# Three blocks of u in batch 0 turned by DMA instead of TensorE, under a new order of all engines

## The chip, the core and the metric

The kernel runs on one core of a Trainium2 chip. The core has a tensor engine (PE, with its weight loads shown apart as PEld), a vector engine (DVE), a scalar engine (ACT), a general engine (POOL) and SyncE (SP), which here issues every DMA. The metric is the device time in microseconds. Before the change the median of four runs is 229.05 us (228.66 to 229.83).

## What is computed

Inputs q, k and v are 4 batches x 8 heads x 768 positions x 64. The first half is a causal attention in which every query sees 6 chunks of 32 keys, those with the highest upper bound of the score. The second half is a mixer on the result, x (4 x 768 x 512).

```
k_min, k_max = min and max of k over each chunk of 32 positions
ub    = sum_d max(q * k_min, q * k_max)           # per query and chunk, causal
sel   = the 6 chunks with the highest ub of each query
attn  = softmax(q k^T / 8, where sel and causal)
x     = attn @ v, heads side by side
theta = x @ w_theta
z_r, z_i = x * cos(theta), x * sin(theta)
y     = w_tok_r @ z_r + w_tok_i @ z_i             # over positions
u     = x + y
out   = u + relu(u @ w_ch)
```

## The kernel before

**A recorded program in a fixed order.** `record` builds a list of some 1,390 operations ("steps" below), each with a name, an engine or a choice of engines, and the tiles that it reads and writes. The string `ORDER` (lines 17 to 77) then says in which order they are issued and, by a letter behind the number, which engine takes a step that several can do: no letter is the first choice, b the second, c the third. `decode` (line 865) turns it into a list and gives each tile its buffer. `F9` stands for nine small matmuls on zeros (line 848) that occupy PE. Each engine works through its own steps in this order, and so does SP with the DMAs: a step that waits holds up all that stands behind it on its engine. The numbers of buffers (`CLASSES`, line 107) matter for the order too: there are 6 input buffers `ld`, shared by q, k, v and weights; the scores have 2 PSUM buffers `sc`; and 3 PSUM buffers `mi` serve almost everything else.

**Names.** A step is named by kind, batch, and pair of heads (0 to 3), head (0 to 7) or block of 128 positions (0 to 5). By stages:

- Loads on SP: `Lq.b.p.x` and `Lk.b.p.x` (line 179, one half of a pair, 192 KB), `Lv.b.p` (line 187, 384 KB), weights `Lwth`, `Lwch`, `Lwtok`. Four of the six blocks of w_tok are turned by DMA (`Twtok`, line 716), the others on PE (`Tw`).
- Turns of q and k on PE, three blocks at a time (`Tq`, `Tk`, lines 231 and 434). Their evictions (`evq`, `evk`, helper lines 169 to 172) go to ACT or DVE; copies in fp16 (`cq`) and the relu of q (`relu`, lines 195 to 199) go to any of three engines.
- Bounds: `red0` and `red1` (lines 240 and 451) reduce k on DVE, `kd` takes the difference, `ub` multiplies on PE (lines 268 to 278, 491). Then DVE does `t1` (transpose), `mx` (nine maxima), `lt` (compare) and `t2` (transpose back). In batches 1 to 3, `cp` (line 536) copies the mask into rows of the q tile, on DVE, ACT or POOL.
- Scores `sc.b.h.s` on PE (line 564; in batch 0 lines 342 and 350), `ex` on ACT (exponential, line 570; 358 in batch 0), `tri` on POOL or DVE (causal triangle, line 580 or 578), `av` on PE (line 402), `norm` on DVE (lines 412 and 413), which writes a head's columns of x.
- Mixer of batch b: x is turned (`Tx` on PE with `evx` in batches 0 and 1, line 608; `Dx` by DMA in batches 2 and 3, line 600). `th.b.t` (line 617) multiplies by w_theta, `sin` and `cos` on ACT (lines 624, 628) need another table of functions than the exponential, `zr` (line 632) makes z on DVE or POOL. `mix.b.t.s` (lines 640 and 642, two matmuls each) adds up y for block t over the six z tiles in turn; `u.b.t` (line 648) adds x on DVE.
- u is turned: on PE by `Tu.b.t` (line 661, four transposes) and an eviction `evu.b.t` on DVE or ACT (line 592 or 593), or by DMA, `Du.b.t` on SP (line 654). The set `U_DMA` (line 97) says which. Then `ch.b.t` (line 673) multiplies by w_ch, `ot` on DVE (line 678) finishes the output block, and `out` on SP stores it (line 683).

The order interleaves the batches: while the mixer of one batch runs, the loads, turns, bounds and scores of the next one are put between its steps.

The two ways of turning u, in the loop over the blocks:

```
if (b, t) in U_DMA:
    op("SP", f"Du.{b}.{t}", 1270, [(u[t], 0)], [(uT[t], 0)],
       lambda t=t: nc.sync.dma_start_transpose(out=T(uT[t]).rearrange("p (c w) -> p c w", w=P), in_=T(u[t])),
       dma=900)
    continue
ps = buf("mi", f"ups.{b}.{t}", (DM,), FP16)
...
op("PE", f"Tu.{b}.{t}", 220, [(u[t], 0)], [(ps, 0)], tr)
ev16(f"evu.{b}.{t}", ps, uT[t], DM)
```

Of the kernel before, what the change touches and what calls it, by code (L numbers as in the profile page):

```python
# [15 lines left out]

ORDER = (
    "10|"
    "3 2 448 4 449b 404b 1 722b 475b 29 28 31 30 0 21 57 17 58 9 18 5 721 19b 14 7 15 56 6 F9 32 20c 10 36 55 "
    "11 35 39 48 12 F17 44 34 13b 8 41 33 85 23 45 75 16c 42 37 47b 38 22 24 84 40 25 F15 50 102 26 68 27 403 "  # L20
    "71 51 69 180 82 52 72 174 181 83 63 175 74 165 65 182 59 64 166 171 49 373 60 374 61 172 168 176b 53 115 "
    "169 67 54 F7 177 173 167b 77 62b 43 46b 170b 178 76c 95 78 125 66 206 179 191 79 96 189 207 103 188 192 "
    "200 80 183 113 208b 201 187 81 193 194 190 184 195 202 90 197 91 203 196 92 198 98 70c 86 73c 141 204 185 "
    "116 88 223 109 199 87 144 99 217 205 186 224 215 126 213 214 211 89 114 209 216 400 226 218 225 399 269 "
    "94 129 101 227 210 127 270 142 220 212 128b 104 133 110c 221 143 228b 219b 145 271 93 105 229 376 272b "
    "106 222 384 137 230 379 375 107 232 402 387 410 100 233 401 108 236 381 97 377 414 386 231 258 412b 380 "
    "234 255 146 385b 130 259 235 237 256 388 246 260 238 239 134 247 240 249 383 257 411b 241 111 250 252 153 "
    "248b 382 253 242 243 251 131 389b 474 378 413 244 273 254 263 132 267 138c 274b 135 245 262 159 266 136b "
    "265 139 268 261 390 140b 264 392 391 418 150 393 275 419 112 416 276 396b 405 394 123 277 417 408 117 "
    "422b 395 407b 162 281 409 278 154 406b 289 415b 147 160 425 155 290 420c 279 285 421c 282 161 280 283 426 "  # L30
    "124 286 435 156 297 427b 287 151 428 119 291 293 284 152 118b 315 288 299 316 429 121 298 317 292 397 295 "
    "301 430 163 302 294 436 437 318 148b 432c 446 308 434c 447 309 296 444 310 445 300 311 319 438 320 431 "
    "149 433 303 157 321 515 439 544 516 120c 304 158 122c 305 440c 347 306 443c 423 348 312 441c 307 468 313 "
    "545 517 471 528 314 343 442b 361 546 470 344b 529 557 164 362 461 463 558 462b 530 554 464b 455 398b 472 "
    "450 559 457b 560 363 465 322 451 459 473 323 452 458 324 467b 466c 494 325 453 456 326 561 454 327 424c "
    "741 345 555 534 328 460b 355 562 535 469 346 349 720 356 518 556 565 350 358 519 357 536b 481 719 359 520 "
    "476 483 563 479 547 482 717 336 477b 548 337 484 745 338 478 549 485 339 746 480 340 341 486b 718 487 342 "
    "489 488 531 495 490 364 743 532 492c 491 353 365 521 493b 541 789 533 522 564 496 742 566 354b 366 542 "
    "523 744 370 497 506 543 786 524 498 526 371 507b 734 736 787 508 329 737 330 735b 372 331 509 739b 332 "
    "499 738 788 333 740b 510 334 765 500 760 511c 335 525 761 360 728 512c 527 351 513c 730 758 352 586 729 "  # L40
    "514c 808 550 501 759 552 551 731 504c 367 587 732 764c 553 723 747 725 810 368 583 748 811 538 727 588 "
    "539 584 369 763 537 750 752 751 606 753 1053 502c 726 580 749 1054 585 755 607 733b 803 540 505c 503c 754 "
    "724b 609 608 804 756 619 762 581 621 620 790 757b 622b 766 591 793 570 792b 610 809 767 813 791b 812 582 "
    "571 794 1056 612 611 768 589 1055 590 613 777 572 573 795 592 769b 574 614 814 832 599 778b 796b 615 575 "
    "617 600 779 567 616 797 601 770 596 568 780 771 597 578 781 569 593 772 784c 576 785b 577 799 598 594 892 "
    "798 774c 618 819 800b 815 776c 898 1079 823 893 801 595 1080 579 775c 1078 899 895 894 816b 1077 802 603 "
    "900 818 885 896 807c 602 817 604 827 820b 623 886 605 882 828 879 897 624 883 903 887 625 822 805 902 880 "
    "626 1057 901 1061 884 631 821 806 904 627 633 1060 881 773 889 1058b 890 888 1059b 853 856 629 891 635 "
    "632 782 783 628 643 634 636 630 637 639 824 644 833c 647 645 638 1075 640 679 646 641 680 681 648 642 651 "
    "649 652 857 653 650 654 682 1076c 683 1120 684 1121 854 825 858 685 869 1099 655 826 855b 697 866 870 831 "  # L50
    "656 829 834 867 657 830 693 1068 835 872 868 1069 844 859 871 672 873 836 845b 837 673 1100b 874 674 846 "
    "658 860 1142 659 838 847 660 839 861 661 848 841b 699 840 851b 849 842 843b 662 852c 700 663 850c 877 701 "
    "875 664 908 918 694 909 1062 1086 1063b 876 919 910 947 1144 1090 675 1145 1089 1064 920 676 878 1087 677 "
    "1088 950 1065 864 862 1066 711 678 702 1067 712 696 1070 703 1094 1071 863 713 1095b 665 704 1073 948 865 "
    "1123 666 1081 1122 1072c 951 1092 1146 934 1084 949 1143b 1147 911 1093b 667 1166 1074 1082 668 1098b "
    "1096c 669 1085 1097 670 912 708 671 1083 1091b 935 924 952b 695 709 1101 925 913b 936b 1137 710 1102 926 "
    "905 1111 1103b 921 1138b 906 1112b 686 1104 1124 922 1135 907 1128 916 944 1105 1136 914 923b 931 1106 "
    "945 1139 915 1125b 705 1141b 917 1140 937 932 1127 687 1108c 706 927 1109c 929 1107b 688 1113 933 707 "
    "1110b 689 946 938 928 1114 1219 930 1167 1126 953 955 1213 1220 1115 939 1129 1214 954 1221 1132 1216 "
    "1117c 1133 941 1119c 1217 942 1131b 690 1215 691 956 1118c 1130 940 1218 1193 692 1226 1134b 1194 1116c "  # L60
    "1161 943 698 1148 1227 1195 1229 1162b 1222 1151 1223 1230 957 1228 1224 1149b 1232 1159 1225 1233 1153 "
    "1231 958 1206 1150 1157 1187 1234 1207 1160b 1236 1237 1156 959 1235 1188 1165c 714 1238 1154 1200 1152 "
    "961 1155 1190 715 1158b 1201 963 1189 1208 960 1191 1168 1163c 1164c 965 962 1202 1203 1169 1192 1198 "
    "1178 971 1170 1179b 716 1171 1196 964 1197 1180 967 972 973 1172 975 966 968 974 969 983 1199 976 979 977 "
    "970 985 1001 978 1002 981 1173 1003 980 1181 1004 1177 984 982 1022 1204 1023 986 1005 1182 994 1176 995 "
    "1184 996 1186 1183 1185b 1006 1174 1175b 1205 1255 1007 1258 1256 1209 1211 1031 1008 1009 1259 1257b "
    "1252 1260 1210 1253 1278 1212 997 1279 1010 1254b 1263 1239 1262 1280 1240 1261 1245 1264 998 1246 1024 "
    "1241b 1271 1025 1247 1272 1265 1026 1273b 1266 1242 1011 1243 1012 1267 1284 1027 1285 1244 1250 1281 "
    "1028 1286 1248 1249 1282 1034 1041 1251 1283 1268 1042 1013 1269 999 1043 1014 1288 1287 1270 1000 1276 "
    "1032 1289 1015 1290 1274 1275 1016 1030 1277 1017 1018 1019 1291 1020 1050 1021 1292 1044 1051 1293 1038 "  # L70
    "1045 987 1039 1294 1297 988 1299 1295 1301 989 1296 990 1298 991 1302 992 1300 1040 1305 1303 1033 993 "
    "1304b 1309 1306 1052 1307 1313 1046 1310 1029 1317 1311 1308 1314 1342 1312 1315 1343 1344 1319 1316 1345 "
    "1318 1335 1320 1336 1337 1338 1339 1340 1346 1341 1347 1328 1365 1348 1329 1330 1331 1366 1321 1322 1323 "
    "1324 1325 1326 1047 1327 1332 1048 1363 1333 1356 1334 1357 1049 1358 1359 1377 1380 1378 1364 1360 1381 "
    "1361 1379 1349 1382 1362 1350 1035 1351 1036 1352 1374 1037 1353 1375 1354 1369 1376 1355 1371 1370b 1367 "
    "1372 1389 1368b 1373 1386 1390 1383 1387 1391 1384 1388 1385 "
)

B, H, S, D = 4, 8, 768, 64
P = 128  # L80
DM = H * D
NT = S // P
CH = 32
NCH = S // CH
QS = 192
NS = S - QS
RUN = NS // 2
# [3 lines left out]
KX = D + NCH  # L91
ROW = (0,)
X_DMA = (2, 3)
K_SB = set()
LAST = (3, 4)
W_DMA = (2, 3, 4, 5)
U_DMA = {(b, t) for b in (1, 2, 3) for t in range(NT) if b < 3 or t < 4}
SEGS = [(0, 4), (1, 3), (2, 5)]
BASE = [0, 1024, 2048]

STEPS = [[(0, 0, 512)], [(0, 512, 256), (4, 512, 256)], [(1, 128, 512)], [(1, 640, 128), (3, 384, 384)],
         [(2, 256, 512)], [(5, 640, 128)]]
OFF = {0: 0, 4: 768, 1: 1024, 3: 1664, 2: 2048, 5: 2560}
# [816 lines left out]
```

## Time and profile before

| | |
|---|---|
| median of four runs | 229.05 us (228.66 to 229.83) |
| the profiled execution | 228.29 us, of which the span of the trace 226.6 us |
| clock granted to PE | 1.0 throughout |
| busy: PE, DVE, ACT, POOL | 216.0, 175.1, 164.8, 94.3 us |
| DMA | 38.06 MB, 71.2% of 16 engines' span on SP's queue |
| first y matmul of batches 0 to 3 | 52.9, 115.3, 167.8 and 199.9 us |

The trace is of one execution, so its durations are used against its own 226.6 us, and 1.7 us lie around that span. The profile's rows of tenths cut the span into 40 slices of 5.7 us; a digit is the busy share of an engine. PE counts as busy while a matmul is in flight, and matmuls overlap, so a row of nines does not say that it works at full rate: a group's mean of 379 ns for a 512-column matmul stands beside 216 ns between two that follow each other. The chain of waits is followed back from the last instruction, at each step to whatever released it. In rows of windows the columns are the window, its length, then busy time with the number of instructions for PE, PEld, DVE, ACT and POOL, the clock, the busy share of the DMA engines, and GB/s.

### The profile page before, as it was taken

Reading aid. Unit: us, or ns where it says so; the run is one execution under the profiler, and the core shown is the slowest. Engines: PE = TensorE matmul, PEld = TensorE weight load, DVE = VectorE, ACT = ScalarE, POOL = GpSimd, SP = SyncE. Lnnn points to the kernel's source line nnn. Section 1 sums busy time; section 2 is a strip of 40 time slices with the busy share of each in tenths; the row PEclk is TensorE's granted clock in tenths of the full one; section 3 lists DMA queues with packets and bytes.
Section 4 is the critical chain, followed back from the end, with each engine's and each line's share of the span. In section 5 each row is a group of like instructions: output and inputs, shape, how many; then the busy total and the mean of one; then the engine's idle time right before and its main releaser. Section 6 shows DMA issues by size and latency. Waiting matters only on the chain.

```text
span 226.6 us, 5663 instructions
## 1 busy us (share of the span) xinstructions
PE 216.0 (95%) x2122; PEld 127.3 (56%) x2122; DVE 175.1 (77%) x505; ACT 164.8 (73%) x247; POOL 94.3 (42%) x190
## 2 busy tenths in 40 slices
PE   7899999999999999888999999999989999999993
PEld 2755766843566658466645565677535564444442
DVE  4599799799979699899986899999885366342553
ACT  2659999999688758999998559899998870560011
POOL 8515557564534648958405314486501130300000
PEclk9999999999999999999999999999999999999999
DMA  7999899999999999986038479514621024662254
GB/s 160 259 258 240 267 303 250 266 319 218 296 241 209 263 247 272 249 195 141 2 72 173 124 122 242 134 48 60 108 48 23 3 69 93 94 186 46 73 173 171
DMA packets 103470, 38.06 MB, mean 168 GB/s; under 512 B 97436, under 2 KB 97820, under 8 KB 103444
## 3 DMA queue, kind: packets, MB, share of 16 engines
q1 hardware_dynamic: 103444, 37.71, 71.2%
q8 instruction: 16, 0.26, 0.5%
q14 instruction: 10, 0.08, 0.1%
HBM read 26.17 MB, written 6.29 MB: 143 GB/s over the span
## 4 chain that ended last, share of the span: by engine, by line
PE 72%; DVE 10%; ACT 8%; DMA 3%; SPq 3%; issue 2%; DVEq 0%; ACTq 0%
PE y L640 13%; PE y L642 13%; PE sc L564 9%; PE ch L673 8%; PE av L402 7%; PE th L617 5%; ACT pt L570 3%; PE qps L434 3%; SPq L600 2%; ACT pt L358 2%; PE kps L434 2%; PE ub L491 2%; DVE km L451 2%; DMA xT<-x 2%; DMA k<-in_k_dram 2%
## 5 line engine op out<-in xcount | busy, mean ns | idle before, releaser
L570 ACT ACTIVATE pt<-sc 128x1024 f16<-128x1024 f32 (+1 forms) x72 | 63.3, 919 | 8.8 <-PE sc L564 8.1
L640 PE MATMUL y<-z,wtokT 128*128 128x512 f16 x144 | 54.6, 379 | 0.1
L642 PE MATMUL y<-z,wtokT 128*128 128x512 f16 x144 | 54.5, 379 | 0.0
L580 POOL TENSOR_SCALAR_AFFINE_SELECT pt<-pt 128x256 f16<-128x256 f16 x62 | 25.6, 417 | 48.9 <-ACT pt L570 47.6
L564 PE MATMUL sc<-qx,kx 88*128 88x512 f16 (+3 forms) x192 | 37.2, 305 | 1.2 <-ACT pt L570 1.0
L402 PE MATMUL av<-v,pt 128*128 128x65 f16 x672 | 30.7, 194 | 1.3 <-ACT pt L570 0.8
L402 PEld LDWEIGHTS <-pt 128*128 128x128 f16 x672 | 27.7, 98 | 7.2 <-ACT pt L570 1.4
L648 DVE TENSOR_TENSOR u<-y,x 128x512 f16<-128x512 f32 x24 | 16.5, 689 | 14.4 <-PE y L642 14.2
L451 DVE TENSOR_REDUCE km<-kps 128x12 f32<-128x384 f32 x48 | 25.1, 546 | 1.5 <-PE kps L434 1.1
L564 PEld LDWEIGHTS <-kx 88*128 88x128 f16 x192 | 16.6, 97 | 13.2 <-issue 2.6
L617 PE MATMUL th<-wtheta,xT 128*128 128x512 f16 x96 | 22.7, 379 | 1.3 <-DMA xT<-x 0.7
L673 PE MATMUL ch<-wch,uT 128*128 128x512 f16 (+1 forms) x96 | 23.6, 374 | 0.0
L642 PEld LDWEIGHTS <-wtokT 128*128 128x128 f16 x144 | 14.1, 98 | 15.1 <-issue 0.9
L640 PEld LDWEIGHTS <-wtokT 128*128 128x128 f16 x144 | 14.0, 97 | 15.1
L678 DVE SCALAR_TENSOR_TENSOR ot<-ch,u 128x512 f32<-128x512 f32 (+1 forms) x24 | 16.3, 678 | 7.5 <-PE ch L673 7.3
L628 ACT ACTIVATE cs<-th,pi 128x512 f16<-128x512 f32 x24 | 16.5, 703 | 6.9 <-PE th L617 6.5
L358 ACT ACTIVATE pt<-sc 128x1024 f16<-128x1024 f32 (+1 forms) x24 | 20.9, 926 | 0.7 <-PE sc L350 0.7
L169 ACT COPY qT<-qps 128x384 f32<-128x384 f32 x24 | 11.2, 486 | 14.0 <-PE qps L231 7.1
L632 DVE TENSOR_TENSOR z<-x,cs 128x1024 f16<-128x1024 f16 x23 | 16.7, 743 | 5.5 <-ACT cs L628 2.7
L172 POOL CAST qx<-qT 64x768 f16<-64x768 f32 (+1 forms) x18 | 14.7, 817 | 11.7 <-ACT qT L169 6.9
L413 DVE TENSOR_TENSOR x<-av,rec 128x384 f16<-128x384 f32 x32 | 17.8, 558 | 1.1
L169 ACT CAST kx<-kps 64x384 f16<-64x384 f32 (+1 forms) x36 | 16.7, 477 | 2.3 <-PE kps L434 1.0
(103 smaller groups left out, 342.1 us busy)
## 6 DMA issues: line engine op xcount, KB each, us to landing
q<-in_q_dram SPq DMA_DIRECT2D x32, 192.0 KB, 3.7
k<-in_k_dram SPq DMA_DIRECT2D x32, 192.0 KB, 3.6
v<-in_v_dram SPq DMA_DIRECT2D x16, 384.0 KB, 4.1
out_dram<-ot SPq DMA_DIRECT2D x23, 256.0 KB, 2.3
wtok<-in_moe_w_tok_r_dram SPq DMA_DIRECT2D x6, 384.0 KB, 4.8
wtok<-in_moe_w_tok_i_dram SPq DMA_DIRECT2D x6, 384.0 KB, 4.6
wth<-in_moe_w_theta_dram SPq DMA_DIRECT2D x4, 256.0 KB, 4.4
wch<-in_moe_w_ch_dram SPq DMA_DIRECT2D x4, 256.0 KB, 4.4
```

Of the source, the lines that this page charges most:

```text
L169: c = {"A": ("ACT", int(n * 0.833 + 60), 0, lambda: nc.scalar.copy(out=out(), in_=in_())), "D": ("DVE", int(n / 0.96 + 70) if psum else in ...
L358: nc.scalar.activation(out=T(pt)[:, :, base:base + w], in_=T(ps).rearrange("p (x c) -> p x c", x=2)[:, :, 0:w], func=AF.Exp, bias=0.0, sca ...
L402: nc.tensor.matmul(ps[:, t, :], T(pt)[:, x, o:o + P], T(v16)[:, x, j, :], start=(j == 0), stop=(j == t))
L413: nc.vector.tensor_tensor(out=T(x16)[:, :, h * D:(h + 1) * D], in0=ps[:, :, 0:D], in1=T(rec).broadcast_to([P, NT, D]), op=ALU.mult)
L451: nc.vector.tensor_reduce(out=T(km)[:, j, 12 * f:12 * f + 12], in_=src.rearrange("p (c w) -> p c w", w=CH), axis=AX.X, op=o)
L564: nc.tensor.matmul(T(ps)[:, a0:a1], T(kx)[0:KX, x, j * P:(j + 1) * P], T(qx)[0:KX, x, q0 + a0 - o:q0 + a1 - o], start=True, stop=True)
L570: nc.scalar.activation(out=T(pt)[:, x, BASE[s]:BASE[s] + w], in_=T(ps)[:, 0:w], func=AF.Exp, bias=0.0, scale=SCALE)
L580: eng.affine_select(out=a, in_=a, pattern=[[0, 2], [1, P]], compare_op=ALU.is_ge, fill=G.zero_reg(), base=0, channel_multiplier=-1)
L617: nc.tensor.matmul(T(ps), T(xT[t])[:, c, :] if by_dma else T(xT[c])[:, t * P:(t + 1) * P], K.wtheta[:, c, :], start=(c == 0), stop=(c == 3))
L640: nc.tensor.matmul(T(ps), K.wtok[:, si, 0, t * P:(t + 1) * P], T(z[si])[:, 0], start=(si == 0), stop=False)
L642: nc.tensor.matmul(T(ps), K.wtok[:, si, 1, t * P:(t + 1) * P], T(z[si])[:, 1], start=False, stop=(si == NT - 1))
L673: nc.tensor.matmul(T(ps)[:, 0:n1 - n0], T(uT[t])[:, c * P:(c + 1) * P], K.wch[:, c, n0:n1], start=(c == 0), stop=(c == 3))
```

## The change

Blocks 3, 4 and 5 of batch 0 join the set whose u is turned by DMA; blocks 0, 1 and 2 of batch 0 and blocks 4 and 5 of batch 3 stay on PE. The whole `ORDER` is another one. Numbers in it shift as well, since a block turned by DMA is recorded as one step and not two.

```diff
 ORDER = (
     "10|"
-    "3 2 448 4 449b 404b 1 722b 475b 29 28 31 30 0 21 57 17 58 9 18 5 721 19b 14 7 15 56 6 F9 32 20c 10 36 55 "
-    "11 35 39 48 12 F17 44 34 13b 8 41 33 85 23 45 75 16c 42 37 47b 38 22 24 84 40 25 F15 50 102 26 68 27 403 "
+    "2 1 28 3 472b 446b 4 31 718 29 30 0 21 5 57 9 58 17 12 14 8 56 18 7 719 15 55 10 401 19b 48 6 20b F21 36 "
+    "32 11 400 16b 41 39b 13b 44 85 37 42 23 83 45 33 47b 34 38 22b 24 82 40b 35 25 F16 50 115 26 68 84 27 71 "
...
-U_DMA = {(b, t) for b in (1, 2, 3) for t in range(NT) if b < 3 or t < 4}
+U_DMA = {(b, t) for b in range(4) for t in range(NT) if (b < 3 or t < 4) and (b, t) not in ((0, 0), (0, 1), (0, 2))}
```

Decoded to names, PE's part around batch 0's mixer reads before (from its third block of y on; `mix.0.3` stands for all six steps of a block):

```
mix.0.3 Tu.0.1 sc.1.1.2 ch.0.0 Tu.0.3 sc.1.0.1 av.1.3.2 ch.0.1 Tk.1.3.1 Tk.1.3.0 av.1.3.0 sc.1.2.2 mix.0.5
Tq.1.3.0 Tq.1.3.1 sc.1.1.1 ch.0.3 Tu.0.5 sc.1.0.2 sc.1.2.0 av.1.3.1 ub.1.2 ch.0.5 av.1.0.0 av.1.0.2 Tq.2.0.0
Tq.2.0.1 mix.0.4 Tq.2.1.1 av.1.0.1 Tk.2.0.1 Tu.0.4 Tq.2.1.0 sc.1.5.2 av.1.2.0 av.1.2.2 av.1.2.1 ch.0.4 Tk.2.0.0
Tk.2.1.0 sc.1.5.1 av.1.1.1 av.1.1.2 av.1.1.0 Tk.2.1.1 sc.1.7.0 sc.1.5.0 Tq.2.2.1 sc.1.7.1 Tx.1.0 ...
```

and after:

```
mix.0.3 Tk.1.3.0 av.1.3.2 Tk.1.3.1 sc.1.1.1 av.1.3.1 sc.1.1.0 av.1.3.0 mix.0.5 (Tq.1.3.1 Tq.1.3.0 before its last)
sc.1.1.2 sc.1.2.0 ch.0.2 ub.1.2 av.1.1.1 sc.1.0.2 mix.0.4 (Tq.2.0.1 Tq.2.0.0 before its last) av.1.1.2 av.1.1.0
Tq.2.1.1 Tq.2.1.0 sc.1.5.2 Tk.2.0.1 Tk.2.0.0 av.1.2.2 av.1.2.1 av.1.2.0 sc.1.5.1 Tk.2.1.1 sc.1.5.0 Tk.2.1.0
av.1.0.0 sc.1.6.2 av.1.0.1 Tk.2.2.0 av.1.0.2 ch.0.3 sc.1.7.1 sc.1.7.2 av.1.5.1 Tx.1.0 Tx.1.1 ... Tq.2.2.1
av.1.7.1 sc.1.6.1 ch.0.5 sc.1.4.0 ch.0.4 Tk.2.3.0 ...
```

SP's part after, around the new DMAs (before, the loads follow each other in much the same way, without a Du):

```
... Lk.2.0.1 Lk.2.1.0 Lk.2.1.1 Du.0.3 Lk.2.2.0 Lk.2.2.1 Lq.2.2.0 out.0.2 Lv.2.1 Lv.2.2 Lk.2.3.0 Du.0.4 Du.0.5
Lq.2.2.1 Lq.2.3.1 Lq.2.3.0 Lk.2.3.1 out.0.3 Lq.3.0.0 ...
```

Steps that changed their engine (before to after): `cp` DVE 14 to 5, ACT 9 to 6, POOL 25 to 37; `evk` and `evq` ACT 60 to 50, DVE 28 to 38; `tri` DVE 17 to 12, POOL 79 to 84; `evu` DVE 4 to 1 (ACT 4, unchanged); fillers on PE 48 to 47; and one or two steps each of casts (`cv`, `cwth`, `cwch`, `cwtok`), `cq`, `relu`, `kd`, `cz`, `qz` and `evw`.

Elsewhere PE's list keeps its shape: the steps of one batch are interleaved with the next in another sequence, and k of the first pair is loaded before its q.

## The prediction

> **What bounds the kernel now.** I read the page first (its sections 1 to 3), then the busy times in slices of 5 us, then the chain of waits from 50 to 120 us, and last the queues. The page says that TensorE is nearly always busy:
>
> ```profile
> PE 216.0 (95%) x2122; PEld 127.3 (56%) x2122; DVE 175.1 (77%) x505; ACT 164.8 (73%) x247; POOL 94.3 (42%) x190
> ...
> DVE  4599799799979699899986899999885366342553
> ACT  2659999999688758999998559899998870560011
> ...
> DMA  7999899999999999986038479514621024662254
> ```
>
> The 95% flatter it. I added up what the orders give PE, with back-to-back prices from the chain (a 512-column matmul 0.216 us, a q or k turn 0.33, an av step 0.19 to 0.29). That is 203.3 us, so some 19 us besides the opening warm-up are waits that the busy row hides. To see where they arise I compare the time of a step with the PE work that stands ahead of it. The difference (I call it the lag) is 6.5 us at the first score step (14.72), 14.0 when batch 0's y matmuls run without gaps (54.71), 18.2 at batch 1's first y matmul (115.32), and 19.5 at the last ch. So 7.5 us are lost before 55 us, 4.2 between 88 and 104, and 1.3 in the last 110 us. Busy times in slices of the middle stretch:
>
> ```profile
> 85.00:90.00 5.00, 5.00 (x80) 4.19 (x79) 4.93 (x13) 4.03 (x8) 4.14 (x7) 1.00 1.08 273
> 90.00:95.00 5.00, 4.13 (x42) 2.53 (x40) 4.39 (x11) 4.90 (x9) 4.70 (x11) 1.00 1.10 266
> 95.00:100.00 5.00, 4.78 (x87) 3.22 (x86) 4.95 (x28) 4.71 (x7) 3.10 (x9) 1.00 1.02 232
> 100.00:105.00 5.00, 3.71 (x48) 2.67 (x49) 4.66 (x13) 4.95 (x8) 3.67 (x10) 1.00 0.35 80
> ```
>
> From 90 us PE (first pair) has gaps while ACT (fourth pair) and DVE (third) are full. The chain of waits agrees: PE and ACT by turns, and ACT the longer.
>
> ```profile
> 60.92 0.22 PE ups L661 x4
> ...
> 89.42 0.92 ACT pt L570
> ...
> 91.24 1.02 ACT pt L570
> ...
> 99.50 1.94 ACT pt L570 x2
> ...
> 103.30 0.93 ACT pt L570
> ```
>
> From 60 to 100 us the DMA queue is full as well (its share is over one, since packets overlap), and the transposes by DMA are seen in the tile view of uT:
>
> ```profile
> q1 hardware_dynamic: 33932, 9.88, 108.5%
> ```
>
> ```profile
> L654 SPq DMA_TRANSPOSE uT<-u x16: 1188/1194/2357, 120.6 to 213.9; - x16
> ...
> DMA to landing us min/median/max: 2.4/2.5/4.2
> ```
>
> **The change, part by part.**
>
> *Turns removed.* Three Tu steps of four transposes leave PE: 3 x 0.23 = 0.69 us, and one filler matmul (48 to 47) 0.07; PE's work falls to 202.55. Three evictions of uT leave DVE, 0.42 each. These lie in the PE-bound stretch 56 to 88 us, but that is followed by the ACT-bound one: by themselves they would only make PE wait longer there. I count them at nothing alone.
>
> *Transposes added.* Three Du, on SP 1.19 us each, landing 2.5 to 4.2 us later. ch.0.3, which needs the first, now stands 17 us of PE work behind its last y matmul, ch.0.5 and ch.0.4 19 and 14 us behind theirs, so the latency is covered. If that cover were gone, each would cost PE up to 4.2 + 1.2 us. Occupancy is another matter. Two windows with little but transposes bound it: 155.1 to 166.1 (six xT and one output, share 0.70) gives at most 1.2 us of all 16 engines for each, and 200 to 214 (share 0.36, three outputs, about five transposes) about 0.6. The Trainium skill (DMA: Bandwidth & Descriptors, "Latency and other measured facts") puts a DMA transpose at 261 GB/s, by which 128 KB would take 0.5 us (an estimate); the same page ("Issuing engines are not separate DMA queues") says that all DMAs share the 16 engines, which speaks against adding any to a full stretch. Sum by the rule 1.5 us, by the rows 1.7 to 3.5; I take 3, since the first window is the more crowded.
>
> *Loads pushed back.* On SP the three Du stand ahead of loads of batch 2. Du.0.3 waits for u.0.3, Du.0.4 for u.0.4; Lk.2.2, Lq.2.2.1, Lq.2.3 and Lk.2.3.1 are queued behind, and PE's turns wait for those. With 0.73 us for a q or k half, 1.46 for a v, 1.0 for an output or a Du (rates of the full stretch), the load most affected is Lq.2.2.1: 88.3 us of transfers up to it before, 93.9 after, while its turn moves from 76.7 to 79.9 us of PE work. Before, it was issued at 85.51, landed by about 89.2 and was used at 91.27: 2.1 us of slack. Net it moves 2.4 us closer, so PE will wait there 0 to 1.5 us. I take 1, and it costs nothing as long as ACT, for which PE then works ahead, is not starved (below).
>
> *Steps moved between engines.* Mask copies (cp) go from DVE (14 to 5) and ACT (9 to 6) to POOL (25 to 37): +5.1 us for POOL at 0.43. Ten evictions of q and k go from ACT to DVE (0.48 there, 0.55 here). Five triangle masks go to POOL. In all DVE loses some 2 us, ACT 1.5, POOL gains 7 on 94. The Trainium skill (SBUF — State Buffer, "Who interferes with whom") says that GpSimd is locked out for the length of a DVE cast in its two-port mode or of one with two SBUF inputs, which speaks against this; the row of the 25 copies is 417/422/523 ns (minimum, median, maximum) among DVE work. By the row 12 copies cost 5.1 us, by the rule up to 0.5 more each, 11. I take the row: the copies are spread over three batches, and POOL, idle for 22% of 85 to 105 us, is not the last.
>
> *The order before batch 1's mixer.* This decides. PE work from batch 1's first y matmul to the end is 106.2 us in both orders, so the time changes by the shift of that start plus later waits. Before, ch.0.3, ch.0.5 and ch.0.4 (2.6 us of PE) run in the PE-bound stretch up to 88 us. After, they stand among the last scores of batch 1, where PE has gaps, and the scores move ahead: sc.1.5.2 has 69.1 us of PE work ahead of it instead of 72.0. PE at lag 14.0 reaches it at 83.2. ACT has first, from the turn of q (81.35), 3.9 us of evictions, a relu and copies, so ex.1.5.2 starts at 85.2 instead of 87.32. From there to the loading of the sine table the page's timeline takes 22.1 us (to 109.43); the new list holds 0.9 more by row prices. That gives 108.2, or 1.2 us earlier. The first y matmul waits for a PSUM buffer that the eighth sine or cosine frees, in both orders, so it too comes 1.2 earlier, at 114.1.
>
> Is DVE late instead? Its t2 of heads 4 to 7 ended at 86.91; after, ub.1.2 starts 1.7 us of PE work earlier and nothing is put between the eight steps, so t2 ends near 82.3. To the first z of batch 1 DVE then has 30.0 us by rows against 27.0 before, which took 26.1 (instructions overlap a little). 82.3 + 29 = 111.3 against 113.02. It is not last, but only by half a us against ACT's shift, and I take 1.1.
>
> *Before 55 us.* k is loaded first instead of q, so the reductions can start some 1.5 us earlier, but q of pair 1 stays ninth on SP and ub.0.0 stands behind it; fillers hold ub.0.1 at 12.6 in both. From there ACT has 0.3 us less and DVE 1.1 less up to the first z, but z.0.1 now waits for seven sines instead of five. I take 0, bounds -0.6 and +0.6.
>
> *After 115 us.* Batch 2's th waits 0.7 us for xT now. Eleven us of turns by DMA (155.1 to 166.1) begin behind the last normalisation of head 6, for which DVE has 0.7 us more to do from ub.3.0 on, while u.1.5 and its Du come 1.6 us of PE work earlier. I take 0, bounds -0.7 (no wait) and +0.7. In the tail ch.2.0 moves ahead to within 0.7 us of its transposed u, and one z goes to POOL (2.12 us) with 1.1 us to spare: 0, up to +0.4.
>
> Sum: -1.1. The profiled execution took 228.29 us, its span 226.6; the span becomes 225.5 and that execution 227.2. It lay 0.76 below the median of the runs, 229.05, and so the forecast is 229.05 - 1.1 = 227.95.
>
> **The rivals.** The measurement can tell some 0.5%, 1.15 us, from no change, so the forecast lies at that edge.
>
> *DVE or PE takes ACT's place* (0.22). For it: DVE is 94 to 99% busy from 85 to 105 and gets evictions. Then only 0.3 +- 0.5 us are won: 228.75, no change.
>
> *More is won* (0.14). The wait for xT goes (-0.7), and the opening keeps DVE's 1.1 less (-0.4): 226.85.
>
> *Loads come late; slower* (0.21). Place: PE's turn of Lq.2.2.1 near 95 us, with the turn of Lk.2.3 right after it. ACT uses that turn at about 97.7, so PE may wait until about 97; from 2 us beyond my estimate of the landing, each us goes straight into the end. With transposes at 2 us each in the crowd, or SP held for a u that DVE makes late, the landing slips by 4 to 5: 227.95 + 2.6 = 230.55. For it: share 1.08 there, issues on SP that already take up to 3.1 us for three. Against: three transposes of wtok between 59 and 68 us did no visible harm.
>
> *The forecast* has 0.43; its own range, 227.3 to 228.6, puts 0.28 beyond the edge. Faster 0.28 + 0.14 = 0.42; slower 0.21 (late loads); same the remaining 0.37. Range 226.7 to 230.4, from the second rival to the third.
>
> **What would show it.** Right: the sine table of batch 1 loaded near 108.2, first y matmul of batch 1 near 114.1, ACT's idle between 60 and 88 us shorter, ch L673 among the scores after 88 us. Wrong: a wait of PE on DMA k or q beyond 1.5 us, DVE ending waits in the chain between 100 and 115, or waits for uT ahead of ch.0.3, ch.2.0 or ch.3.2.

## The result and the profile after

The changed kernel took 228.57 us (median of 36 runs, 226.69 to 230.59), the kernel before 229.17 (55 runs taken with them): a ratio of 0.9975, 95% interval 0.996 to 0.999. It is faster by 0.6 us, about half of the 1.1 that was forecast; the direction and the range held, the size did not, and the runs below show that the 0.6 us are not made where the forecast made its gain. A few runs (two of the 36, 230.34 and 230.59 us) are slow ones, more than 1.5% above the fastest of their kernel, and all ratios leave them out.

The profiled execution took 228.71 us, its span 227.0. That is 0.4 us more than the span shown of before, although the kernel is faster: before's execution lay 0.9 below its median, this one 0.1 above. Two single spans therefore settle nothing here, and I compare stretches inside the executions, and over several executions with the same list of steps. The page first, its rows of engines and its slices:

```profile
PE 216.6 (95%) x2109; PEld 126.5 (56%) x2109; DVE 171.2 (75%) x493; ACT 163.6 (72%) x240; POOL 103.0 (45%) x206
...
DVE  3699869769689999999988998899693436434353
ACT  2779799999585769999996389889997880560011
...
DMA  6999899999999999979366369405510313543333
```

DVE and ACT gave work to POOL as listed (POOL 94.3 to 103.0). The busy times of 85 to 105 us, to be laid beside those of before, with the same columns (PE first pair, DVE third, ACT fourth):

```profile
85.00:90.00 5.00, 4.43 (x50) 3.13 (x49) 4.64 (x12) 4.90 (x9) 4.57 (x8) 1.00 0.94 229
90.00:95.00 5.00, 4.59 (x65) 3.31 (x65) 4.94 (x11) 4.90 (x10) 4.67 (x11) 1.00 0.90 195
95.00:100.00 5.00, 5.00 (x81) 3.28 (x80) 4.68 (x26) 4.95 (x9) 2.38 (x8) 1.00 0.78 193
100.00:105.00 5.00, 5.00 (x69) 3.56 (x67) 4.80 (x16) 4.80 (x8) 3.33 (x8) 1.00 1.03 253
```

PE's gaps have shrunk and moved ahead, as the forecast wanted, and ACT is full from 85 on instead of from 90. But in the chain of waits (start, length, what) a new row stands far ahead of that stretch:

```profile
52.55 2.52 DVE z L632 x3
...
56.49 1.88 POOL qx L536
58.36 0.04 issue
58.41 1.03 PE sc L564 x6
```

A mask copy that POOL has taken over from VectorE holds the first scores of batch 1. It is the longest of its group by far (minimum, median, maximum in ns):

```profile
L536 POOL COPY qx<-nsT x37: 416/420/1867, 56.0 to 172.6; 24x288 f16<-24x288 f16 x37
```

The median is what the forecast charged. The one copy of 1.87 us is over four times that, and PE waits for it. The DMA queue is as full as before from 60 to 85 us and less full from 85 to 100 (shares of 0.94, 0.90 and 0.78 in the rows above, against 1.08, 1.10 and 1.02). The three transposes did no visible harm here: in the tile view of uT from 75 to 105 us PE's longest idle time ahead of a ch is 0.4 us, and none of it ends with a landing. Nor does any wait of PE from 55 to 118 us end with a landing of q or k, so the forecast's third rival, late loads, did not come.

```profile
L654 SPq DMA_TRANSPOSE uT<-u x3: 1258/1265/1394, 80.6 to 90.7; - x3
...
its engine sat idle before it (us, times) until:
  issue: 0.4, 1
  DVE km L451: 0.3, 1
```

To say where time was won or lost, three stretches of the trace: up to the first y matmul of batch 0, from there to the first y of batch 1, and from there to the end of the last matmul. All times in us, one profiled execution each; the ratio is of the timed runs to runs of before taken in the same set, with its 95% interval.

| kernel | to first y of 0 | to first y of 1 | to the end | ratio to before |
|---|---|---|---|---|
| before | 52.86 | 62.46 | 107.69 | 1 |
| changed | 52.80 | 62.79 | 107.73 | 0.9975 (0.996 to 0.999) |
| e1 mask copy on VectorE | 51.16 | 61.70 | 107.30 | 0.9935 (0.991 to 0.996) |
| e9 POOL's copies swapped | 51.91 | 62.37 | 107.75 | one run, 227.4 us |
| e12 a product moved | 52.46 | 61.66 | 107.50 | one run, 227.0 us |
| e4 mask copy and cast | 51.06 | 61.06 | 107.79 | 0.9913 (0.988 to 0.995) |
| e8 two copies off ScalarE | 52.47 | 60.77 | 107.50 | 0.9917 (0.989 to 0.995) |
| e10 and a cast in the opening | 52.06 | 60.97 | 107.78 | 0.9909 (0.988 to 0.994) |
| e2 turns on PE | 52.11 | clock low | 107.08 | 1.011 (1.007 to 1.015) |
| e3 turns on PE, ch ahead | 52.38 | 67.35 | 106.77 | 1.0175 (1.013 to 1.022) |
| e5 before, turns by DMA | 52.79 | 63.41 | 108.85 | 1.0102 (1.006 to 1.014) |
| e11 before, ch later only | 52.80 | 63.02 | 107.82 | 1.0029 (1.001 to 1.005) |
| e6 new opening, old rest | 55.14 | 62.46 | 108.27 | 1.0147 (1.010 to 1.020) |
| e7 old opening, new rest | 53.63 | 62.80 | 107.13 | 1.0056 (1.003 to 1.008) |

The middle column repeats to 0.01 us where the list of steps is the same (before and e6; changed and e7), so it can be read to a tenth. That rests on two pairs. The first column of the new opening scatters, 51.06 to 52.80 over the eight executions that have the same steps up to there (all of the changed list but e10; mean 52.0); that of the old is 52.8 or 52.9 in three.

### The profile page after: what moved, and what is told of

The parts are those of the page before. It is cut to its first block, busy times and chain, and to the rows that moved or that the text cites. A ratio compares the mean times of both kernels' runs of the same rounds, so it can differ in the third digit from the quotient of the medians.

```text
span 227.0 us, 5650 instructions
## 1 busy us (share of the span) xinstructions
PE 216.6 (95%) x2109; PEld 126.5 (56%) x2109; DVE 171.2 (75%) x493; ACT 163.6 (72%) x240; POOL 103.0 (45%) x206
## 4 chain that ended last, share of the span: by engine, by line
PE 67%; ACT 8%; DVE 8%; DMA 8%; SPq 3%; issue 2%; POOL 1%; DVEq 0%; ACTq 0%; POOLq 0%
PE y L640 13%; PE y L642 13%; PE sc L564 10%; PE ch L673 7%; PE av L402 7%; PE th L617 5%; ACT pt L358 4%; DMA wth<-in_moe_w_theta_dram 3%; PE qps L434 3%; SPq L600 2%; PE kps L434 2%; DMA uT<-u 2%; PE ub L491 2%; DMA xT<-x 2%; DMA q<-in_q_dram 2%
## 5 line engine op out<-in xcount | busy, mean ns | idle before, releaser
L580 POOL TENSOR_SCALAR_AFFINE_SELECT pt<-pt 128x256 f16<-128x256 f16 x65 | 26.5, 413 | 37.2 <-ACT pt L570 36.3
L536 POOL COPY qx<-nsT 24x288 f16<-24x288 f16 x37 | 17.8, 483 | 14.9 <-DVE nsT L528 13.3
L632 DVE TENSOR_TENSOR z<-x,cs 128x1024 f16<-128x1024 f16 x23 | 16.3, 721 | 6.1 <-ACT cs L628 3.3
L169 ACT CAST kx<-kps 64x384 f16<-64x384 f32 (+1 forms) x31 | 14.4, 473 | 7.1 <-PE kps L231 4.6
L624 ACT ACTIVATE cs<-th 128x512 f16<-128x512 f32 x24 | 14.1, 617 | 7.2 <-PE th L617 7.1
```

The lines of the kernel that those rows point to most:

```text
L536: eng(out=T(qx)[D:KX, x, QS + r * run:QS + (r + 1) * run], in_=flat(nsT)[w0:w0 + NCH, 0:run])
L580: eng.affine_select(out=a, in_=a, pattern=[[0, 2], [1, P]], compare_op=ALU.is_ge, fill=G.zero_reg(), base=0, channel_multiplier=-1)
```

## The experiments

Edits are given in names of steps; in the files they are numbers in `ORDER`. In the kernels of e1 to e4, e8 and e10 the lines of `record` stand three lower than elsewhere (L533 is L536, L629 is L632).

**e1, the mask copy alone.**

```diff
-mx.1.0.1/DVE mix.0.2.1/PE cp.1.0.0.1.1/POOL cp.1.0.0.0.1/ACT ... cp.1.0.0.0.0/POOL
+cp.1.0.0.0.0/DVE mx.1.0.1/DVE mix.0.2.1/PE cp.1.0.0.1.1/POOL cp.1.0.0.0.1/ACT ...
```

> The changed kernel with one mask copy of batch 1's first head (cp.1.0.0.0.0) on VectorE, ahead of the maxima mx.1.0.1, instead of on POOL, where it took 1.87 us beside VectorE's z products; nothing else. Theory A (the forecast gain of 85 to 115 us is made, but PE was already 1.6 us later from 58 us on, 1.3 of it this one copy): the copy takes 0.23 us, the first score of batch 1 starts near 57.1 instead of 58.41, ex.1.5.2 near 86.4 instead of 87.66, batch 1's first y near 114.3 instead of 115.58, and the time falls by a further 1.0 to 1.3 us, a ratio to before of about 0.992. Theory B (ScalarE or VectorE are last from 85 us whatever PE does before, the gain is simply smaller than forecast): the first score is earlier, but the first y of batch 1 stays within 0.3 us of 115.6 and the ratio near 0.997.

The copy in the timeline (start, length, engine, line):

```profile
54.28 0.23 DVE L533 COPY qx<-nsT 24x288 f16<-24x288 f16 x1
```

From first y to first y it took 61.70 us instead of 62.79, and the ratio fell from 0.9975 to 0.9935 (two sets of runs, whose intervals just meet). Theory A holds: the 1.1 us won at 58 us are still there at 113 us. One step of some 1,400, on the wrong engine for its moment, cost about as much as the whole change was to bring.

**e9 and e12, why the copy was slow.** In e9 VectorE's list is unchanged and POOL's two copies change places; in e12 POOL's list is unchanged and one product of VectorE moves.

```diff
 e9:
-cp.1.0.0.1.1/POOL ... cp.1.0.0.0.0/POOL
+cp.1.0.0.0.0/POOL cp.1.0.0.1.1/POOL
 e12:
-sin.0.5/ACT mx.1.0.1/DVE ... zr.0.5/DVE
+sin.0.5/ACT zr.0.5/DVE mx.1.0.1/DVE
```

> The changed kernel with POOL's first two mask copies of batch 1 in the other order: cp.1.0.0.0.0 first, cp.1.0.0.1.1 second; VectorE's list unchanged. Theory L (POOL stands still while VectorE runs its products and compares of two SBUF inputs; so the price goes with the place in time, not with the copy): the first copy, beside the maxima, takes 0.42 us, the second, beside z.0.5, lt.1.0.1 and z.0.4, 1.87; the first score no longer waits, the second does, and from batch 0's first y to batch 1's it takes 62.4 us instead of 62.8. Rival (the copy itself is slow, by its buffer or its rows): cp.1.0.0.0.0 takes 1.87 again, and nothing changes.

> The changed kernel with POOL's list unchanged and one step of VectorE's moved: the product z.0.5 ahead of the nine maxima mx.1.0.1 instead of behind them. Theory L: now the first of the two POOL copies meets z.0.5 and takes about 0.9 us, the second meets the maxima and takes 0.42; together 1.3 to 1.4 us instead of 2.29, the first score of batch 1 about 0.9 us earlier against batch 0's first y, and 62.0 us instead of 62.8 between the two first y. Rival (DMA writes or POOL's own start make the copy slow): 2.3 us for the two again.

The timeline of the changed kernel, first POOL, then VectorE beside it:

```profile
56.49 1.87 POOL L536 COPY qx<-nsT 24x288 f16<-24x288 f16 x1
```

```profile
56.50 0.67 DVE L632 TENSOR_TENSOR z<-x,cs 128x1024 f16<-128x1024 f16 x1
57.09 0.38 DVE L523 TENSOR_TENSOR ns<-ubT,t 128x216 f16<-128x216 f32 x1
57.39 0.68 DVE L632 TENSOR_TENSOR z<-x,cs 128x1024 f16<-128x1024 f16 x1
57.99 0.47 DVE L528 STREAM_TRANSPOSE nsT<-ns 128x288 f16<-128x288 f16 x1
```

The copy starts 0.01 us ahead of a product and ends when three instructions of two SBUF inputs, one close behind the other, are over (58.07) and some 0.3 us more have passed. In e9 the other copy stands in that place, and it is now the slow one:

```profile
55.62 1.86 POOL L536 COPY qx<-nsT 24x288 f16<-24x288 f16 x1
```

In e12 the first copy meets the product and the second the maxima:

```profile
55.69 0.73 POOL L536 COPY qx<-nsT 24x288 f16<-24x288 f16 x1 [1.49 <-DVE nsT L528]
```

```profile
56.46 0.42 POOL L536 COPY qx<-nsT 24x288 f16<-24x288 f16 x1
```

Theory L holds in both: the price goes with what VectorE does at that moment, not with the copy. The stretch between the two first y was 62.37 (62.4 expected) and 61.66 (62.0 expected). In e9 only the second pair's scores wait, 0.4 us less; in e12 the two copies together take 1.15 us instead of 2.29.

**e4, the same in the other direction.** In the changed kernel the product z.0.2 took 1.31 us beside a POOL cast that began 0.15 us earlier, and PE stood idle for 0.64 us ahead of its third step of y.

```profile
53.01 0.92 POOL L172 CAST wtok<-wtok 128x768 f16<-128x768 f32 x1 [0.68 <-PE th L617]
53.16 1.31 DVE L632 TENSOR_TENSOR z<-x,cs 128x1024 f16<-128x1024 f16 x1
54.52 0.38 PE L640 MATMUL y<-z,wtokT 128*128 128x512 f16 x1 [0.64 <-DVE z L632]
```

```diff
 (as e1, and)
-cz.1.0.1/DVE cwtok.1.3/POOL t2.1.0.0/DVE ... cp.1.0.0.1.1/POOL cp.1.0.0.0.1/ACT Lq.1.2.0/SP
+cz.1.0.1/DVE t2.1.0.0/DVE ... cp.1.0.0.1.1/POOL cp.1.0.0.0.1/ACT cwtok.1.3/POOL Lq.1.2.0/SP
```

> As the run with one mask copy on VectorE, and the POOL cast cwtok.1.3 moved behind POOL's first mask copy, so that it no longer runs beside the product z.0.2, which took 1.31 us instead of 0.68 and held PE's third y step by 0.9 us. Theory A: z.0.2 takes 0.7, the lag of PE at the first score of batch 1 is about 13.7 instead of 15.64, the first y of batch 1 near 113.8, the time 1.6 to 1.9 us below the changed kernel's, ratio about 0.990. Theory B: whatever is won before 60 us is waited away by 115 us, ratio near 0.997. Risk: Lq.1.2.0, which reuses the cast's buffer, is issued 2 us later, and PE's turn of it at 65.3 may then wait.

In e4 the same three products in a row, to be read against the 2.52 us of the chain above:

```profile
50.82 1.90 DVE L629 TENSOR_TENSOR z<-x,cs 128x1024 f16<-128x1024 f16 x3
```

0.62 us less, and the stretch shrank by 0.64 more, to 61.06. The ratio, 0.9913, is as expected within its interval; theory B falls again. PE's turn of Lq.1.2.0 did not wait.

**e8 and e10, what is last then.**

```diff
 e8 (e4, and):
-cp.1.2.1.0.1/ACT ... cq.2.0.1/ACT ... ex.1.7.0/ACT tri.1.4.1/POOL
+cp.1.2.1.0.1/POOL ... ex.1.7.0/ACT cq.2.0.1/POOL tri.1.4.1/POOL
 e10 (e8, and):
-cwth.0/ACT ... Lwtok.0.1/SP ... ex.0.2.3/ACT
+ex.0.2.3/ACT cwth.0/ACT Lwtok.0.1/SP
```

> As the run with the mask copy on VectorE and the cast moved (226 us, 0.9913), with two more copies taken from ScalarE: the mask copy cp.1.2.1.0.1 to POOL, right behind its neighbour, and the copy of q cq.2.0.1 to POOL, ahead of tri.1.4.1 where POOL idles. 1.26 us less for ScalarE, which is busy without a gap from 82 to 106 us. If ScalarE is last there, as the forecast's deciding step had it: the first y of batch 1 comes 0.8 to 1.2 us earlier relative to th of batch 0, ratio about 0.987. If VectorE is as near to being last as the forecast's first rival said: 0 to 0.3 us, ratio 0.990 to 0.992.

> The run with fewer copies on ScalarE (0.9917), and in the opening one more step moved: the cast cwth.0 on ScalarE, which waited up to 1.1 us at 27 us for its weights to land while the exponentials behind it were ready, goes behind the exponential ex.0.2.3, and the load Lwtok.0.1, which takes its buffer, behind it. Expected: the wait on the weights is gone, PE's lag at sc.0.2.0 rises by 1.4 us from ub.0.2 in every execution instead of 1.4 to 2.6, and the median falls by 0.3 to 0.6 us: ratio about 0.989. Rival: the load Lwtok.0.1 lands later and PE's turn of that weight waits instead; ratio 0.992 or above.

1.26 us less of ACT brought 0.3 between the two first y, and no change in the runs. Both copies stood ahead of ex.1.5.2, and ACT now waits there for PE instead, once for a turned k and once for an av:

```profile
84.53 0.48 ACT L166 CAST kx<-kps 64x384 f16<-64x384 f32 x1 [0.76 <-PE kps L431]
85.25 0.70 ACT L567 ACTIVATE pt<-sc 128x640 f16<-128x640 f32 x1 [0.25 <-PE av L399]
```

With the copies cured, ACT is no longer alone in being last ahead of ex.1.5.2; PE is next, as the forecast's first rival had it. In e10 the stretch from ub.0.2 to sc.0.2.0 took 10.9 us, against 11.8 in the changed kernel's execution, where the cast waited 1.39 us for its weights. But it took 10.7 in that of e1, which has the changed kernel's steps there and whose cast waited 0.30, so one execution does not show a gain, and the ratio, 0.9909, cannot be told from 0.9917 and 0.9913. e1, e4, e8 and e10 all beat both kernels: the last three lie 0.8 to 0.9% below before and some 0.6% below the changed kernel's ratio. Which of them is best stays open.

**e2 and e3, the turns and ch undone.**

```diff
 e2 (changed kernel, and):
-U_DMA with (0,3), (0,4), (0,5): Du.0.3 Du.0.4 Du.0.5 on SP
+U_DMA of before: Tu.0.3 evu.0.3/DVE ahead of av.1.2.2, Tu.0.4 evu.0.4/DVE ahead of ex.1.5.0,
+Tu.0.5 evu.0.5/DVE ahead of Tx.1.0
 e3 (changed kernel, and):
+Tu.0.3 evu.0.3/DVE ahead of mix.0.4.0, Tu.0.5 evu.0.5/DVE behind av.1.1.2, Tu.0.4 evu.0.4/DVE ahead of Tk.2.0.1
+ch.0.3 ahead of av.1.1.2, ch.0.5 ahead of Tq.2.1.1, ch.0.4 ahead of sc.1.5.1, each with its ot and out
```

> The changed kernel's order, but u of blocks 3, 4 and 5 of batch 0 turned by PE and evicted by VectorE again, after the last q and k turns of batch 2's first pairs and ahead of the same ch steps; the three transposes by DMA gone. Theory A, as in the forecast: the turns are worth nothing by themselves, so the ratio stays at 0.9975 within 0.002, and the first y of batch 1 moves by less than 0.4 us. Theory B: the DMA turns are what gains; then 0.7 us of PE and 1.2 of VectorE return and the ratio goes to 1.000 or above. Theory C: their occupancy in a full queue costs; then this is faster by 0.3 to 0.5% than the changed kernel and PE's waits for k and q get shorter.

> As the kernel with the turns on PE, but with ch of blocks 3, 5 and 4 moved back ahead of batch 1's scores of heads 4 and 5 (0.3 and 0.5 ahead of sc.1.5.2, 0.4 ahead of sc.1.5.1), their relu-adds and outputs with them. The forecast's deciding step says: sc.1.5.2 gets 2.1 us more of PE work ahead of it, ex.1.5.2 comes 1.5 to 2 us later than in the changed kernel (about 89.4), the first y of batch 1 about 1.2 later (116.8), ratio 1.002 to 1.004. Rival: PE's gaps after 88 us take it up and ScalarE is not last; then ex.1.5.2 is later, but the first y is at 115.6 to 116.0 and the ratio within 0.002 of the changed kernel's.

Both were far slower than expected. e2 is 1.35% above the changed kernel (3.1 us), where the forecast had the turns at nothing: theories A and C fail, and of B the direction came, at more than its price. Part of the 3.1 us may be the clock. In four of the five runs of e2 that enter its ratio the mean clock granted to PE was 0.990 or 0.991, in the changed kernel's 0.997 or more; the fifth, at 0.999, took 229.77 us, which would be 2.4 us above the changed kernel. Of e2's trace I use only who waited for whom, since its clock was low in parts (0.69 from 60 to 65 us, 0.88 from 90 to 95). At 58 us, where its list is still the changed kernel's, that execution also lost some 1.5 us that have nothing to do with the turns: the mask copies on POOL stand behind a cast, which waited 4.05 us for a block of w_tok to land, and PE waited 2.42 us for the copy instead of 0.96. The turns themselves:

```profile
91.66 0.38 PE L658 MATMUL ups<-ident,u 128*128 128x128 f16 x4 [0.71 <-DVE km L448]
92.56 0.55 PE L431 MATMUL kps<-ident,k 128*128 128x128 f32 x3 [0.52 <-DVE uT L589]
```

A turn on PE needs one of three PSUM tiles. It waits until DVE has reduced a k out of one, and the next k turn waits until DVE has evicted u. e3, whose clock was 1.0, shows the second of these waits as well:

```profile
89.23 0.55 PE L431 MATMUL kps<-ident,k 128*128 128x128 f32 x3 [0.31 <-DVE uT L589]
```

In a stretch where DVE is 95% busy (85 to 105 us of the changed kernel) that is a longer path than the 0.69 us of PE. How much of the loss a better place for the turns would save was not tried. Between e2 and e3 the timed difference is 0.65% (1.5 us), as much as the forecast's deciding step gave to moving ch behind the scores; but the turns stand in other places too, and the interval of that difference reaches nearly to 0, so this supports it and does not show it.

**e5 and e11, the turns by DMA in the old order.**

```diff
 e11 (before, and):
+ch.0.5 ot.0.5 ahead of av.1.0.1, ch.0.4 ot.0.4 out.0.4 ahead of Tx.1.0, out.0.5 behind Lv.2.2
 e5 (e11, and):
-Tu.0.3 evu.0.3 Tu.0.5 evu.0.5 Tu.0.4 evu.0.4
+Du.0.3 ahead of Lq.2.0.1, Du.0.5 ahead of Lq.2.2.1, Du.0.4 ahead of Lv.2.2
```

> The kernel before with its own order and engines, but u of blocks 3, 4 and 5 of batch 0 turned by DMA (three transposes on SP in the place of PE's twelve and three evictions), and, so that the landing is covered, ch.0.5 moved some 4 us later (ahead of av.1.0.1) and ch.0.4 some 8 us (ahead of Tx.1.0), each with its relu-add and output. The run with the turns put back on PE was 1.35% slower than the changed kernel, against a forecast of nothing. If the turns on PE cost a PSUM buffer and a round trip through VectorE in the full stretch (theory A), taking them away gains here too: PE's lag from 84 to 115 us, 4.0 us before, falls to 3 or less, ratio 0.995 or below. If the loss was my placing of them in the changed order (theory B), the ratio is 1.000 within 0.003. If transposes and loads collide (theory C), PE waits for q at Lq.2.2.1's turn and the ratio is 1.005 or more.

> The kernel before with ch.0.5 and ch.0.4, their relu-adds and outputs moved later exactly as in the run of its order with turns by DMA (1.0102), but the turns left on PE. Is the 1% there the price of the DMA turns or of the moved steps? Theory D (three transposes in a queue that is full): ratio 1.000 to 1.003, so 0.7% or more belongs to the DMA. Theory P (ch.0.5 then waits for a PSUM buffer that VectorE frees, and the buffers come round in another order): ratio 1.006 or more, and PE's wait ahead of ch.0.5 is 0.5 us or more here too.

Moving the ch steps alone costs 0.3%, with the turns by DMA it is 1.0%. So theory D has the larger part: in this list the three transposes cost about 0.7%, with an interval from 0.3 to 1.2. Theory P fails: the ch.0.5 of e11 does not wait. In e5 it does, and for the landing of its transposed u:

```profile
84.46 0.33 PEld L673 LDWEIGHTS <-uT 128*128 128x128 f16 x3 [0.88 <-DMA uT<-u]
84.47 0.60 PE L673 MATMUL ch<-wch,uT 128*128 128x512 f16 x2 [0.65 <-DVE u L648]
```

In a ch the block uT is what PE loads as weights. The second line names DVE's u, but in the trace DVE signals that at 84.48, behind the start, and the DMA issued at 79.84 signals its landing at 84.42. So here ch.0.5 stood too near its transpose, by some 0.65 us.

Theory A fails outright, and of theory C the ratio came but not the place: PE does not wait for q at Lq.2.2.1's turn. Of the 1.4 us between the two profiled executions only 0.4 lie between the two first y, where that wait stands; 1.0 lies behind, at longer waits for the xT of batches 2 and 3. Whether the transposes caused those is not shown.

**e6 and e7, the openings exchanged** at the q turn Tq.1.0.1, about 43 us.

```diff
-ORDER of one kernel
+ORDER of changed up to Tq.1.0.1, with Tk.1.1.1 and its four followers put ahead of it,
+then all steps not yet done in the order of before (e6); the reverse, with Tk.1.1.0 (e7)
```

> The changed kernel's order for all that it has ahead of the q turn Tq.1.0.1 (about the first 43 us of PE: k loaded first, other fillers, other engines for the copies), then the rest in the order and on the engines of the kernel before, turns on PE. Where do the 0.25% of the whole change come from? Theory O (from the opening, which the forecast put at nothing): ratio 0.997 to 0.998, th of batch 0 earlier than in the executions of the kernel before by about 0.6 us. Theory M (from 85 to 115 us, half of it given back at 54 to 58): ratio 1.000 within 0.002.

> The counterpart: the kernel before up to the q turn Tq.1.0.1, then the changed kernel's order with its turns by DMA, its copies on POOL and the one mask copy at 56.5 us among them. Theory O: ratio 1.000 within 0.002. Theory M: ratio 0.997 to 0.998. If both parts gain and this and its counterpart are both below 0.9975 or both above, the parts do not add, and what the profile shows at th of batch 0, at the first score of batch 1 and at the first y of batch 1 says where.

Neither theory's number came, because the seam itself costs: ahead of the next turn, Tq.1.1.1, PE stands idle for 1.97 us in e6 and 1.88 in e7, a wait that the profile puts down to no releaser. The ratios are of no use for the question, but the middle column is: 62.46 and 62.80, that is, each rest of the list takes there what it takes in its own kernel, whatever opened it. The middle therefore did not gain by the change. It lost 0.33 us. And e7, with the old opening and the new rest, is not faster than before: its first y of batch 0 is 0.8 us late, and all that follows takes 0.2 us less than before's. That fits theory O, but since the seam cannot be priced, these two runs do not show it.

## Where the forecast was right and where it failed

The 0.6 us come from other places than forecast, and that the direction came out right is in good part luck: the gain lies in the two stretches that the forecast put at nothing.

| stretch | forecast | measured in the traces |
|---|---|---|
| to the first y of batch 0 | 0 (-0.6 to +0.6) | -0.8 (52.8 in three executions to a mean of 52.0 in eight) |
| to the first y of batch 1 | -1.1 | +0.33 (62.46 to 62.79) |
| from there on | 0 (-0.7 to +0.7) | -0.5 (107.7, 107.8, 108.3 in lists of before, e11 and e6; 106.8 to 107.8 in nine with the changed list, e2 left out, mean 107.5) |

The sum is -1.0, just beyond what the runs say (-0.2 to -0.9 by the interval); the first and the third line scatter by more than that difference.

**The step that failed: "I take the row: the copies are spread over three batches, and POOL ... is not the last."** The row (417/422/523 ns) was right for 33 of the 37 copies, and the sum over all is small: a mean of 483 ns against 427, 2.1 us of POOL in all. But 1.45 of these lie in one copy. The row was taken where the copies stood before, and the change put this one beside VectorE's products, ahead of the scores that open batch 1. It was slow because of what VectorE did beside it (e9, e12), and PE waited for it: e1 gave back 1.1 us by the first y of batch 1. The Trainium skill (SBUF — State Buffer, "Who interferes with whom") had spoken against it: VectorE instructions with two SBUF inputs and GpSimd share ports and exclude each other. I weighed it as an addition to twelve copies, 0.5 us each, instead of asking of each moved copy what VectorE does at that moment and who waits. By the rule for the one copy, with the three rows beside it, 0.42 + 0.67 + 0.38 + 0.68 = 2.15 us could have been written down (an estimate from the rows); it measured 1.87.

**The same rule the other way round** cost 0.6 us at z.0.2 (e4). It had no line in the forecast at all; before's trace already showed two products of 1.30 us, beside POOL casts, which cost PE no idle time above 0.2 us there.

**The deciding step itself** is right in its mechanism. It said that from ex.1.5.2 on ACT is last, and that the first y of batch 1 moves with it. From ex.1.5.2 to that y it is 28.0 us before and 27.9 in the changed kernel, e1, e4, e7, e9 and e12 (28.2 or 28.3 in e5, e10 and e11): where ex.1.5.2 goes, the first y goes. In the changed kernel ACT is busy for 27.5 of the 27.9 us, DVE and PE for 27.1 each, so ACT is last by little. The forecast put 28.9 (0.9 for added ACT work, which did not show). What was wrong is the start: "PE at lag 14.0 reaches it at 83.2", so that ACT has its turn of q at 81.35 and ex.1.5.2 starts at 85.2. Both came 2.5 us later, and the sine table 1.5 later than forecast:

```profile
83.90 0.86 ACT L169 COPY qT<-qps 128x384 f32<-128x384 f32 x2 [1.12 <-PE qps L434]
87.66 0.70 ACT L570 ACTIVATE pt<-sc 128x640 f16<-128x640 f32 x1
109.73 1.28 ACT L628 ACT_TABLE_LOAD   x1
```

Of the 2.5 us, e1 returns 1.1 and e4 another 0.6; the other 0.8 stay open, since the trace of e4 shows no idle time of PE above 0.2 us between the first y and that score. In e4 the middle takes 1.4 us less than before, a little more than the 1.2 that the forecast had for this step: the gain was in the new order, and two waits had spent it before it was made.

**"Before 55 us: 0"** looks wrong by 0.8. Half of that is firm: from th.0.0 to the first y it takes 7.2 us in the three executions with before's list (7.6 in e6) and 6.8 in those with the changed order (6.95 in e2; e7, which has the changed order there, 6.8 too). Before, th.0.5 waited 0.6 us for the PSUM tile that DVE's first transpose of batch 1 frees, in the changed kernel 0.2; in the new order the copies cq.1.1.0 and cq.1.1.1 no longer stand ahead of that transpose. This was the second rival's "the opening keeps DVE's 1.1 less (-0.4)". The other half lies between 0 and 45 us and scatters with the landing of q and of the weights; its cause stays open. "After 115 us" the wait of batch 2's th for xT seems some 0.4 us shorter on average, again a term of that rival; the executions scatter by more, and it was not tested by itself.

**The turns.** "I count them at nothing alone" is not borne out: e2 puts their return at 2.4 to 3.1 us and e5 (against e11) their removal at a loss of 1.7, each in a list that was not made for it. What a turn on PE costs there is the wait for a PSUM tile and for DVE, on top of its 0.23 us; of what the turns by DMA cost in e5, a wait of 0.65 us for a landing is seen, and the rest is not traced to one place. Both prices hold for these lists alone, and the sum by single parts could not have given them. Of the forecast's signs of being right only one came, ch among the scores after 88 us, which the order itself gives. The table load (109.73 for 108.2) and the first y of batch 1 (115.58 for 114.1) failed, and ACT's idle time between 60 and 88 us did not shrink (6.8 us before, 7.0 after).

## What to carry to other kernels

When a step changes its engine, do not price it by the mean of its row: look up what the engines that share ports with it are doing at the moment where it lands, and who waits for it. In a list that several in-order engines share, compare the time of a step with the work ahead of it, engine by engine, since a loss at 58 us shows as a late exponential at 88. And moving a few steps of such a list cost 0.3 to 1.4% here (e11, e5, e2), so a part that is undone singly tells the price of the part only if the trace shows that nothing else has begun to wait.

## What the runs showed of the hardware

In the changed kernel and in e9 POOL got no turn between VectorE instructions of two SBUF inputs that follow each other closely: a copy of 0.42 us took 1.87 and 1.86 beside three of them, until the third was over, and 0.73 beside the one of e12. VectorE was held up as well: its product took 0.69 us alone and up to 1.31 beside a POOL cast that had begun first (e4). Beside VectorE's maxima, reductions and transposes the POOL copy kept its 0.42 in the changed kernel. And the time to the first y of batch 0 scattered by 1.7 us between executions of the same steps, while the 62 us that follow repeated to 0.01 in two pairs.
